# Tying GpSimd's token-number write to the place where its batch is placed, in a spectral-filter plus mixture-of-experts kernel

## The chip, the cores and the metric

The kernel runs on one core of one Trainium2 chip. The metric is the device time of one execution in microseconds (us), less is better; three runs of the kernel before stand as its measurement.

## What is computed

The input is eight batches of 2496 rows by 256 columns. Each batch is filtered in the frequency domain, and every filtered row (a token, 19968 in all) goes through one of eight experts:

```python
X = np.fft.rfft(x, axis=1)
y = np.fft.irfft(X * (filt_r + 1j * filt_i)[None], n=2496, axis=1)
t = y.reshape(19968, 256)
logits = t @ w_gate + modality_bias[modality_id]
e = argmax(logits, axis=1)                  # one expert of 8
gate = softmax(logits)[arange(N), e]
out = gate[:, None] * (relu(t @ w1[e]) @ w2[e])
```

## The kernel before

**Stages.** The transforms are matrix products on TensorE (PE): stage 1, then stage 2 (forward, filter on VectorE, inverse), then stage 3, with two DRAM tensors `b1_d` and `b2_d` between them for the later batches. Stage 3 of batch g fills a row tile `yw` (`yo0` for even g, `yo1` for odd g, in the order listings `yo_105` and `yo_106`) of 128 partitions by 20 rows. A row of it is 130 words: 128 words hold the 256 fp16 values of a token, one word its token number, and one its gate weight.

**Routing.** After stage 3 of a batch, `counting(g)` on VectorE (DVE) finds each token's expert and a running count `c`. `placing(g)` has PE sum `c` over the partitions (`psO`, lines 637 and 638), and DVE works out from it the row `pos_i` of each token in the bins (line 652). At its head GpSimd (POOL) writes the 2560 token numbers of the batch into the row tile: `tok` plus `g * S`, line 635, once for each batch. `scatter(g, t)` (line 678) then sends column t of the row tile into `bins_d` in DRAM by an indirect DMA that POOL issues; there are 20 of these for each batch, 160 in all. They are called bins-scatters below.

**Experts.** The bins are read back in blocks of 256 tokens of one expert (`xs`, issued by SyncE). `turn` transposes a block (`pT`, then DVE's copy `xT`, line 786) and copies the expert's first matrix (line 777); `up` (line 799) and `down` (line 812) are the two products, in four steps a block. At the end of a block DVE multiplies by the gate into `osb` (line 819, twice a block), and POOL issues two indirect DMAs that put the rows into the output (line 821, the out-scatters). `osb` has three buffers: DVE may write the one of block k + 3 when the out-scatters of block k have landed. `ops`, the sum in PSUM, has two.

**Order.** All engines run their instructions in the order of their queues. In the main loop (lines 1136 to 1170) each turn n does a step of stages 1 to 3 of several batches, one or two bins-scatters (`pace`) and 1.5 steps of experts. The order in each queue is made at build time by a scheduler that looks at dependences. An instruction on POOL that depends on nothing recent may be put far ahead of its place in the program. To hold DMAs back, the kernel has `paced` (line 130), which adds a dependence on the last PE matmul that was recorded so far in `marks["pe"]`:

```python
def paced(ins):
    tc.add_manual_dep(ins.ins, marks["pe"][-1].name, ..., reason="pace")
```

Weight loads (line 450), some x loads and the bins-scatters (line 686) are paced. Line 635 is not: it depends on `tok` and on the row tile alone. Its first two executions have nothing to wait for but the set-up use of these tiles. From batch 2 on it waits until the bins-scatters of batch g - 2, which read the same row tile, have landed in DRAM.

Of the kernel before, what the change touches and what calls it, by code (L numbers as in the profile page):

```python
# [16 lines left out]
ALU = mybir.AluOpType  # L17
# [12 lines left out]
def kernel(  # L30
# [12 lines left out]
    nc = tc.nc  # L43

    B, S, D = x.shape
# [31 lines left out]
    DW = D // 2  # L77
# [52 lines left out]
    def paced(ins):  # L130
        tc.add_manual_dep(ins.ins, marks["pe"][-1].name,
                          mybir.DependencyInfo(mybir.DependencyClass.Sync, mybir.DependencyReason.DATA),
                          reason="pace")
# [18 lines left out]
    op = ctx.enter_context(tc.tile_pool(name="opsum", bufs=1, space=bass.MemoryType.PSUM))  # L152
# [477 lines left out]
    def placing(g):  # L630

        yw, lg = st[g]["yw"], st[g]["lg"]
        b3 = [P, NY, E]
        mx, ohT, sc, c = st[g]["route"]
        nc.gpsimd.tensor_single_scalar(yw[:, :, DW:DW + 1], tok, g * S, op=ALU.add)
        psO = pp.tile([P, 2, E], F32, tag="ps")
        nc.tensor.matmul(psO[:, 0, :], lhsT=Lexcl, rhs=c, start=True, stop=True)
        nc.tensor.matmul(psO[:, 1, :], lhsT=ones_sq, rhs=c, start=True, stop=True)
        nc.vector.tensor_sub(lg, lg, mx[:, :, None].to_broadcast(b3))
        nc.scalar.activation(lg, lg, AF.Exp)  # L640
        off = sp.tile([P, E], F32, tag="off")
        nc.vector.tensor_add(off, cnt, ecap)
        nc.vector.tensor_add(off, off, psO[:, 0, :])
        nc.vector.tensor_add(cnt, cnt, psO[:, 1, :])
        yield
        nc.vector.tensor_add(sc, sc, off[:, :, None].to_broadcast([P, E, NY]))
        nc.vector.tensor_mul(sc, sc, ohT)
        yield
        pos = sp.tile([P, NY], F32, tag="pos")
        nc.vector.reduce_sum(pos, sc.rearrange("p e t -> p t e"), axis=AX.X)  # L650
        pos_i = sp.tile([P, NY], I32, tag="posi", bufs=2)
        nc.vector.tensor_copy(pos_i, pos)
        st[g]["pos"] = pos_i
        yield
        ssum = sp.tile([P, NY], F32, tag="ssum")
        nc.vector.reduce_sum(ssum, lg, axis=AX.X)
        nc.vector.reciprocal(yw[:, :, DW + 1].bitcast(F32), ssum)
# [10 lines left out]
    def place(g):  # L668

        run(placing(g))  # L670
# [277 lines left out]
    with tc.manual_schedule(engines={ET.PE, ET.Activation, ET.DVE}):  # L948
# [92 lines left out]
        tok = const_pool.tile([P, NY, 1], I32)  # L1041
# [36 lines left out]
        def routes(g):  # L1078

            yield from counting(g)  # L1080
            for _ in range(4):
                yield
            yield from placing(g)
            to_bins.append([g, 0])
            yield
            yield from tabling(g, KR[g], False)
# [127 lines left out]
```

## Time and profile before

| what | value |
|---|---|
| three runs, median (lowest to highest) | 594.89 us (594.38 to 596.47) |
| the profiled execution's own time | 592.98 us |
| its span, first to last instruction | 591.2 us |
| busy: PE, DVE, ACT, POOL | 512.1, 377.6, 379.9, 367.4 us |
| granted TensorE clock, mean share of full speed | 0.941 |
| bins-scatters (line 678) | 160, mean 1013 ns |
| out-scatters (line 821) | 158, mean 1014 ns |
| token-number writes (line 635) | 8, 3.1 us busy, 21.3 us idle ahead of them |

A busy time is the sum of an engine's instructions. Idle time is put down to what ended it. The clock is the share of full speed that TensorE was granted; 1.0 is 2.4 GHz and 0.5 is 1.2 GHz.

### The profile page before, as it was taken

How to read it: one execution, taken by the hardware profiler on the slowest of the kernel's cores; microseconds unless marked ns; L12 is line 12 of the kernel's file. 1: busy time of each engine (PE TensorE's matmuls, PEld its weight loads, DVE VectorE, ACT ScalarE, POOL GpSimd, SP SyncE). 2: the span in 40 equal slices, each digit the busy share in tenths (PEclk: the TensorE clock that was granted, in tenths of full speed). 3: DMA queues.
4: the chain of work that ended last, by engine and by line, in shares of the span. 5: the costliest groups of instructions: out<-in, count | busy, mean ns of one | idle time of the engine just before them, and what ended most of it. 6: DMA issues, size and time to landing. Idle time of an engine off the chain costs nothing.

```text
span 591.2 us, 16242 instructions
## 1 busy us (share of the span) xinstructions
PE 512.1 (87%) x5115; PEld 463.2 (78%) x5115; DVE 377.6 (64%) x1209; ACT 379.9 (64%) x693; POOL 367.4 (62%) x409
## 2 busy tenths in 40 slices
PE   3689986739969989999999989966999999999991
PEld 2677875628858888888888978855999999999991
DVE  8557986656766777769679777554555555555541
ACT  4578886827856877777876754433666666666660
POOL 8112336727746776774776776777777777655552
PEclk9969998969998998999998999978999999999997
DMA  8949999887697787898667463224444443333321
GB/s 152 184 68 192 197 212 208 180 204 209 160 239 208 203 198 222 231 211 241 184 176 204 139 165 112 87 86 146 137 127 123 119 125 122 118 109 110 99 73 33
DMA packets 69301, 93.29 MB, mean 158 GB/s; under 512 B 11427, under 2 KB 52841, under 8 KB 69059
## 3 DMA queue, kind: packets, MB, share of 16 engines
q0 software_dynamic: 21504, 50.75, 35.2%
q1 hardware_dynamic: 24409, 29.94, 20.1%
q10 hardware_dynamic: 23302, 11.50, 7.4%
q8 instruction: 48, 0.79, 0.6%
q14 instruction: 38, 0.31, 0.2%
HBM read 64.68 MB, written 46.35 MB: 188 GB/s over the span
## 4 chain that ended last, share of the span: by engine, by line
PE 46%; DMA 20%; issue 11%; POOL 9%; DVE 8%; ACT 3%; SPq 0%; POOLq 0%; DVEq 0%; ACTq 0%
PE hps L799 14%; PE ops L812 13%; POOL out_dram L821 5%; DMA t<-b_d 5%; DMA b_d<-t 3%; DMA bins_d<-yo,pos_i 3%; DMA b_d<-z 3%; PE ps L476 3%; DMA out_dram<-osb,meta 2%; DMA g<-g 2%; PE pz L488 2%; PE lt L584 2%; PE ps L569 2%; PE pz L489 2%; PE pT L785 2%
## 5 line engine op out<-in xcount | busy, mean ns | idle before, releaser
L804 ACT ACTIVATE hT<-hps 128x512 f16<-128x512 f32 x316 | 188.1, 597 | 120.7 <-PE hps L799 118.7
L799 PE MATMUL hps<-xT,w 128*128 128x256 f16 x1264 | 203.6, 282 | 5.7 <-DVE xT L786 5.6
L821 POOL DMA_INDIRECT out_dram<-osb,meta x158 | 160.1, 1014 | 76.4 <-DVE osb L819 36.6
L812 PE MATMUL ops<-w2sb,hT 128*128 x1264 | 198.5, 277 | 2.7 <-issue 2.5
L678 POOL DMA_INDIRECT bins_d<-yo,pos_i x160 | 162.1, 1013 | 56.6 <-issue 19.8
L799 PEld LDWEIGHTS <-w 128*128 128x128 f16 x1264 | 148.1, 146 | 11.0 <-DVE xT L786 6.0
L812 PEld LDWEIGHTS <-hT 128*128 128x128 f16 x1264 | 125.2, 99 | 18.9 <-issue 3.1
L819 DVE TENSOR_SCALAR osb<-ops,meta 128x256 f32<-128x256 f32 x158 | 69.4, 475 | 24.9 <-DMA out_dram<-osb,meta 17.3
L777 DVE COPY w<-w1sb 128x2048 f16 x79 | 56.2, 711 | 42.9 <-PE hps L799 41.1
L786 DVE COPY xT<-pT 128x512 f16<-128x512 f16 x79 | 33.4, 423 | 53.0 <-PE pT L785 52.3
L503 ACT CAST xf<-ps 104x512 f16<-104x512 f32 x96 | 56.9, 592 | 11.5 <-PE ps L476 9.5
L510 DVE TENSOR_TENSOR p<-xf,g 104x512 f16<-104x512 f16 x96 | 40.5, 421 | 36.7 <-ACT xf L503 35.8
L525 ACT CAST z<-pz 104x512 f16<-104x512 f32 x72 | 42.5, 590 | 9.7 <-PE pz L489 8.1
L476 PE MATMUL ps<-t,w2m 104*104 104x256 f16 x192 | 39.9, 292 | 8.7 <-DMA t<-b_d 7.9
L511 DVE TENSOR_TENSOR xf<-xf,g 104x512 f16<-104x512 f16 x96 | 40.5, 421 | 10.0 <-DMA g<-g 6.9
L488 PE MATMUL pz<-p,a1m 104*104 104x256 f16 x144 | 37.5, 284 | 2.7 <-DVE p L510 1.8
L218 ACT CAST t<-ps 96x512 f16<-96x512 f32 x52 | 30.1, 581 | 14.3 <-PE ps L214 12.8
L593 DVE COPY yT<-lt 128x512 f16<-128x512 f16 x80 | 33.5, 419 | 7.1 <-PE lt L589 6.3
L489 PE MATMUL pz<-xf,a2m 104*104 104x256 f16 x144 | 36.6, 280 | 0.0
L785 PE MATMUL pT<-ident,xs 128*128 128x128 f16 x316 | 32.8, 227 | 4.4 <-DMA xs<-bins_d 4.4
L144 POOL DMA_DIRECT2D xt<-in_x_dram x32 | 18.3, 573 | 28.7 <-PE fp L253 14.2
L584 PE MATMUL lt<-ident,yo 128*128 128x128 f16 x320 | 31.4, 221 | 3.7 <-ACT z L525 3.3
(206 smaller groups left out, 725.5 us busy)
## 6 DMA issues: line engine op xcount, KB each, us to landing
xs<-bins_d SPq DMA_DIRECT2D x79, 130.0 KB
xt<-in_x_dram POOLq DMA_DIRECT2D x24, 384.0 KB
t<-b_d SPq DMA_DIRECT2D x18, 384.0 KB
t<-b_d SPq DMA_DIRECT2D x15, 416.0 KB
b_d<-z ACTq DMA_DIRECT2D x30, 208.0 KB
b_d<-t ACTq DMA_DIRECT2D x24, 192.0 KB
w1sb<-in_moe_w_dram POOLq DMA_DIRECT2D x16, 256.0 KB
w2sb<-in_moe_w_dram POOLq DMA_DIRECT2D x8, 512.0 KB
```

Of the source, the lines that this page charges most:

```text
L476: mm = nc.tensor.matmul(ps[:KB, i, :], lhsT=w2m[:, s + i, :], rhs=st[g]["t2", s // SCH][:, s % SCH + i, :], start=True, stop=True)
L488: nc.tensor.matmul(pz[:KB, i, :], lhsT=a1m[:, s + i, :], rhs=p1[:, i, :], start=True, stop=False)
L489: nc.tensor.matmul(pz[:KB, i, :], lhsT=a2m[:, s + i, :], rhs=p2[:, i, :], start=False, stop=True)
L503: nc.scalar.copy(xf, ps[:KB])
L678: ins = nc.gpsimd.indirect_dma_start(out=bins_d[:, :], out_offset=IOA(ap=st[g]["pos"][:rows, t:t + 1], axis=0), in_=st[g]["yw"][:rows, t, ...
L777: cp = nc.vector.tensor_copy(b["w1"].rearrange("p a f -> p (a f)"), w1sb[:, ds(ej, 1)].rearrange("p o a f -> p (o a f)"))
L785: nc.tensor.transpose(pT[:, dc, i, :], xh[:, i, dc * P:(dc + 1) * P], ident)
L799: mm = nc.tensor.matmul(hps[:, k, :], lhsT=b["w1"][:, dc, ft:F:FT], rhs=b["xT"][:, dc].rearrange("p i t -> p (i t)"), start=(dc == 0), sto ...
L804: nc.scalar.activation(b["hT"][:, q * FQ:(q + 1) * FQ, :], hps, AF.Relu)
L812: nc.tensor.matmul(b["ops"][:, i, :], lhsT=b["hT"][:, ft, i * P:(i + 1) * P], rhs=w2sb[:, ds(b["ej"], 1), ft, :], start=(ft == 0 and i == ...
L819: nc.vector.tensor_scalar_mul(osb[:, i, :], b["ops"][:, i, :], gate[:, i, :])
L821: ins = nc.gpsimd.indirect_dma_start(out=out[:, :], out_offset=IOA(ap=b["meta"][:, i, 0:1], axis=0), in_=osb[:, i, :], in_offset=None, bou ...
```

## The change

The write of the token numbers gets the same dependence as the bins-scatters: it waits for the last PE matmul that was recorded before its batch was placed. Nothing else in the program is changed.

```diff
@@ placing(g) @@
         mx, ohT, sc, c = st[g]["route"]
-        nc.gpsimd.tensor_single_scalar(yw[:, :, DW:DW + 1], tok, g * S, op=ALU.add)
+        paced(nc.gpsimd.tensor_single_scalar(yw[:, :, DW:DW + 1], tok, g * S, op=ALU.add))
         psO = pp.tile([P, 2, E], F32, tag="ps")
```

The queues of PE, DVE, ACT and SyncE hold the same instructions in the same order as before, with waits on the same semaphores. Only POOL's queue differs. In the pieces below, rows with a minus are of the kernel before and rows with a plus of the changed one; the bracket names the semaphores that an instruction waits for (DMASW0 to DMASW7: DMAs that POOL issued; PE, DVE, Activation, Pool: these engines).

POOL's queue where the bins-scatters of batch 3 (from `yo_106`) end and those of batch 4 (from `yo_105`) begin:

```order
 L678 DMA bins_d<-yo_106,pos_i 162048x130 [waits DMASW2_49,PE_49]
-L635 TENSOR_SCALAR yo_106<-tok 128x20 [waits DMASW6_49,DMASW5_49,DMASW7_49,DMASW4_49,DMASW2_49]
 L144 DMA xt<-in_x_dram 96x512 [waits DMASW3_49,PE_49]
-L821 DMA out_dram<-osb,meta 19968x256 [waits DVE_49]
-L678 DMA bins_d<-yo_105,pos_i 162048x130 [waits DVE_49,PE_49,Pool_49]
-L678 DMA bins_d<-yo_105,pos_i 162048x130
+L635 TENSOR_SCALAR yo_105<-tok 128x20 [waits PE_49]
+L821 DMA out_dram<-osb,meta 19968x256 [waits DMASW4_49,DVE_49]
+L678 DMA bins_d<-yo_105,pos_i 162048x130 [waits DMASW5_49,DVE_49,Pool_49]
+L678 DMA bins_d<-yo_105,pos_i 162048x130 [waits DMASW6_49]
```

Before, the write that stands here is the one of batch 5, into the tile that batch 3 has just been sending out, and it waits for five DMA semaphores. In the changed queue it is the write of batch 4, into the other tile, and it waits for PE.

POOL's queue where batch 5 (`yo_106`) ends and batch 6 (`yo_105`) begins:

```order
 L678 DMA bins_d<-yo_106,pos_i 162048x130 [waits DMASW7_49]
-L635 TENSOR_SCALAR yo_106<-tok 128x20 [waits DMASW5_49,DMASW6_49,DMASW2_49,DMASW7_49,DMASW1_49,DMASW0_49]
-L821 DMA out_dram<-osb,meta 19968x256 [waits DVE_49] x2
-L678 DMA bins_d<-yo_105,pos_i 162048x130 [waits DVE_49,PE_49,Pool_49]
+L635 TENSOR_SCALAR yo_105<-tok 128x20 [waits PE_49]
+L821 DMA out_dram<-osb,meta 19968x256 [waits DMASW0_49,DVE_49]
+L821 DMA out_dram<-osb,meta 19968x256 [waits DMASW1_49,DVE_49]
+L678 DMA bins_d<-yo_105,pos_i 162048x130 [waits DMASW2_49,DVE_49,Pool_49]
```

Here the write of batch 7 gives its place to the write of batch 6. The same holds one batch earlier, where batch 4 ends and batch 5 begins.

POOL's queue where the bins-scatters of batch 6 have ended and those of batch 7 begin:

```order
 L821 DMA out_dram<-osb,meta 19968x256 [waits DMASW6_49,DVE_49]
 L821 DMA out_dram<-osb,meta 19968x256 [waits DMASW7_49,DVE_49]
-L821 DMA out_dram<-osb,meta 19968x256 [waits DMASW0_49,DVE_49]
-L821 DMA out_dram<-osb,meta 19968x256 [waits DMASW1_49,DVE_49]
-L678 DMA bins_d<-yo_106,pos_i 162048x130 [waits DVE_49,DMASW2_49,PE_49,Pool_49]
+L635 TENSOR_SCALAR yo_106<-tok 128x20 [waits PE_49]
+L821 DMA out_dram<-osb,meta 19968x256 [waits DMASW0_49,DVE_49]
+L821 DMA out_dram<-osb,meta 19968x256 [waits DMASW1_49,DVE_49]
+L678 DMA bins_d<-yo_106,pos_i 162048x130 [waits DMASW2_49,DVE_49,Pool_49]
```

Before, no write stands here any more. In the changed queue the write of batch 7 comes here, ahead of the out-scatters of one block.

## Rows read from the trace of the kernel before

**Rows 1.** The page, busy time and share of the span of each engine.

```profile
PE 512.1 (87%) x5115; PEld 463.2 (78%) x5115; DVE 377.6 (64%) x1209; ACT 379.9 (64%) x693; POOL 367.4 (62%) x409
```

**Rows 2.** Who waited for whom, POOL, 181 to 504 us: total, times, longest.

```profile
POOL yo L635 <- DMA bins_d<-yo,pos_i: 16.4, 4, 6.4
...
POOL out_dram L821 <- DVE osb L819: 7.6, 24, 0.5
```

**Rows 3.** The timeline of POOL: start, duration, instruction, idle time before and its releaser.

```profile
124.70 0.29 POOL L635 TENSOR_SCALAR yo<-tok 128x20 int32<-128x20 int32 x1 [4.74 <-DMA bins_d<-yo,pos_i]
130.12 1.05 POOL L678 DMA_INDIRECT bins_d<-yo,pos_i  x1 [5.13 <-DVE take L737]
...
276.06 0.32 POOL L635 TENSOR_SCALAR yo<-tok 128x20 int32<-128x20 int32 x1 [6.41 <-DMA bins_d<-yo,pos_i]
...
277.47 1.30 POOL L821 DMA_INDIRECT out_dram<-osb,meta  x1 [0.30 <-DVE yT L593]
...
320.25 0.28 POOL L635 TENSOR_SCALAR yo<-tok 128x20 int32<-128x20 int32 x1 [2.72 <-DMA bins_d<-yo,pos_i]
...
323.65 0.97 POOL L678 DMA_INDIRECT bins_d<-yo,pos_i  x1 [0.30 <-PE pT L785]
...
363.74 0.28 POOL L635 TENSOR_SCALAR yo<-tok 128x20 int32<-128x20 int32 x1 [2.89 <-DMA bins_d<-yo,pos_i]
...
367.13 0.98 POOL L678 DMA_INDIRECT bins_d<-yo,pos_i  x1 [0.30 <-PE lt L589]
...
394.90 1.02 POOL L821 DMA_INDIRECT out_dram<-osb,meta  x1 [0.30 <-DVE xT L786]
...
404.07 1.00 POOL L821 DMA_INDIRECT out_dram<-osb,meta  x1 [0.30 <-issue]
...
434.02 0.98 POOL L821 DMA_INDIRECT out_dram<-osb,meta  x1 [0.30 <-DVE meta L789]
```

**Rows 4.** Who waited for whom, whole span: the waits of DVE's gate product.

```profile
DVE osb L819 <- DMA out_dram<-osb,meta: 17.3, 8, 5.5
```

**Rows 5.** The timeline of DVE: gate products and the bins' positions.

```profile
271.66 0.47 DVE L819 TENSOR_SCALAR osb<-ops,meta 128x256 f32<-128x256 f32 x1
...
315.53 0.17 DVE L652 CAST pos_i<-pos 128x20 int32<-128x20 f32 x1
...
355.79 0.17 DVE L652 CAST pos_i<-pos 128x20 int32<-128x20 f32 x1
...
384.67 0.88 DVE L819 TENSOR_SCALAR osb<-ops,meta 128x256 f32<-128x256 f32 x2 [4.41 <-DMA out_dram<-osb,meta]
...
399.00 0.88 DVE L819 TENSOR_SCALAR osb<-ops,meta 128x256 f32<-128x256 f32 x2 [2.37 <-DMA out_dram<-osb,meta]
...
407.95 0.88 DVE L819 TENSOR_SCALAR osb<-ops,meta 128x256 f32<-128x256 f32 x2 [5.51 <-DMA out_dram<-osb,meta]
...
427.83 0.86 DVE L819 TENSOR_SCALAR osb<-ops,meta 128x256 f32<-128x256 f32 x2
```

**Rows 6.** The timeline of PE: placing's sums, and the first matmuls after its idle times.

```profile
311.25 0.28 PE L637 MATMUL psO<-c,Lexcl 128*128 128x8 f32 x2
...
350.83 0.39 PE L637 MATMUL psO<-c,Lexcl 128*128 128x8 f32 x2 [0.66 <-DVE c L627]
...
388.80 0.60 PE L637 MATMUL psO<-c,Lexcl 128*128 128x8 f32 x2 [5.33 <-DVE c L627]
...
401.28 0.66 PE L799 MATMUL hps<-xT,w 128*128 128x256 f16 x4 [1.18 <-DVE xT L786]
...
409.37 1.07 PE L799 MATMUL hps<-xT,w 128*128 128x256 f16 x4 [3.94 <-DVE xT L786]
```

**Rows 7.** Busy time in stretches: length, PE (matmuls), PEld, DVE, ACT, POOL, clock, DMA.

```profile
389.00:396.00 7.00, 7.00 (x42) 5.73 (x43) 3.82 (x20) 1.84 (x4) 5.39 (x6) 0.59 0.25 77
...
410.00:416.00 6.00, 6.00 (x36) 4.71 (x34) 1.71 (x6) 2.07 (x4) 4.48 (x6) 0.56 0.48 149
416.00:450.00 34.00, 34.00 (x327) 31.78 (x325) 18.71 (x48) 21.56 (x37) 26.07 (x27) 1.00 0.41 124
```

## The prediction

> **What bounds the kernel now.** I read the busy times first, then POOL's waits, then the timelines of POOL, DVE and PE side by side. By busy time PE is the engine that counts, with 87% of the span against 62% for POOL [rows 1]. That is an average over stages. Between 181 and 504 us POOL works through its queue without a pause worth the name: 24 waits for `osb` come to 7.6 us with none over 0.5 us, which is the 0.30 us step from one DMA to the next. The one exception is the token-number write, 16.4 us in four waits, each for the bins-scatters just issued to land [rows 2]. So in this stretch POOL is behind, and whatever holds it makes it later still.
>
> Who suffers? DVE writes `osb` into three buffers and waits for the out-scatter of three blocks earlier. These waits are 17.3 us in 8 times in the whole run [rows 4], and the three long ones lie at 385, 399 and 408 us, with 4.41, 2.37 and 5.51 us [rows 5]. DVE runs in order, so its stand at 385 us delays the count `c`, on which PE then stands for 5.33 us; the other two delay `xT`, on which PE stands for 1.18 and 3.94 us [rows 6]. After the first and the third the granted clock is 0.59 and 0.56 for a while, the lower level for most of it, and from 416 us on it is 1.00 with PE busy throughout [rows 7]. This is where time can be had.
>
> How late is POOL? Blocks leave DVE and POOL in the same order, so I count pairs. The `osb` of 384.67 us [rows 5] is the pair of out-scatters issued from 404.07 us [rows 3]: 19 us behind. Late in the run, where PE is never idle, the pair of 427.83 us is issued at 434.02 us, 5.3 us after its DVE instruction pair ends.
>
> **The change, part by part.** *The write itself* stays on POOL, eight times some 0.3 us [rows 3]: nothing gained or lost. *Its wait for landed scatters* goes: the write of batch g now stands at the head of batch g, and the scatters that read the same tile were those of batch g - 2, a whole batch earlier. *The added wait* is for a PE matmul recorded before the batch is placed, so it should have run before `psO`. Behind it in POOL's queue stand an x load or out-scatters, and then the bins-scatters. `psO` ran at 311.25 and 350.83 us [rows 6]; POOL came to the places at 317.5 and 360.9 us (320.25 less 2.72, 363.74 less 2.89 [rows 3]). Even if POOL comes 8 us sooner, the wait is over, so I cost it at nothing; what it costs if PE is later is the slower rival below.
>
> *What each removed wait frees on POOL.* The 4.74 us at 120 us are followed by 5.13 us for DVE's positions [rows 3]; that is late next, so zero. The fourth wait of rows 2 is 16.4 less 6.41, 2.72 and 2.89, so 4.4 us; it is over before any `osb` wait, since the first of the three long ones is at 380 us: zero. The three others add up, each up to what is late next:
> - At batch 4 the pair of 277.47 us cannot go before its `osb`, 271.66 plus 0.47 us [rows 5], plus 0.3: 272.4 us. POOL gains 5.1 us of the 6.4.
> - At batch 5 the gain would be 5.1 + 2.72 + 0.3, but the first bins-scatter (323.65 us) needs `pos_i`, ready at 315.70 us. With 0.3 it goes at 316.0 us: the gain is 7.7 us.
> - At batch 6 another 2.89 + 0.3 us give 10.9; the first scatter (367.13 us) needs `pos_i` of 355.96 us, so at best 356.3 us: 10.8 us.
>
> From there POOL's row of DMAs is the same as before, 10.8 us earlier.
>
> *What DVE and PE get from it.* The first stand (4.41 us) needs only 4.4 of the 10.8 us and vanishes. PE's 5.33 us shrink to 0.9, a gap about as long as the 0.66 and 1.18 us ones. The slow clock goes with it: 42 matmuls took 7.00 us where the later stretch needs 34.00 / 327 = 0.104 us each, so 4.4; that gives 2.6 us [rows 7]. Together 7.0. The second stand then comes at 399.00 - 2.37 - 7.0 = 389.6 us, and its buffer is free at 399.00 - 10.8 = 388.2: it vanishes, and PE's 1.18 us too. The third comes at 407.95 - 5.51 - 7.0 - 1.2 = 394.2, but its buffer is free only at 407.95 - 10.8 = 397.1 us: 2.9 of the 5.51 us stay. DVE waits have cost PE some 1.2 to 1.6 us less than their length (2.37 to 1.18, 5.51 to 3.94), so PE stands some 1.3 us, 2.6 less, without the slow stretch of 36 matmuls in 6.00 us, another 2.3. PE is ahead by 7.0 + 1.2 + 2.6 + 2.3 = 13.1 us at 416 us.
>
> But POOL is ahead by only 10.8, so its lag of 5.3 us would become 7.6. How much can three buffers bear? A buffer is free some 4 us after its pair is issued (394.90 to 399.00, 404.07 to 407.95 [rows 3, 5]). At 36 matmuls a block a block takes 3.74 us (0.104 x 36), three take 11.2, less 0.9 for the product itself and 4.0: an estimate of 6.3 us. So about 1.0 to 1.5 us of the 13.1 are given back in small `osb` waits: 10.8 + 6.3 - 5.3 = 11.8 is the ceiling. I take **11.5 us**. From there on PE is the bound in both kernels, and the gain stands to the end.
>
> *Both ends.* What no row shows is how POOL behaves when it is no longer behind: it may then wait for the PE marks of the bins-scatters. The low end is the first stand alone, 7.0 us. The high end is every PE row named, 4.4 + 2.6 + 1.2 + 3.9 + 2.3 = 14.4 us. I sit nearer the ceiling since by these sums POOL still lags by 3 us and more from 360 us on.
>
> **The numbers.** The profiled execution took 592.98 us, 1.8 around its span of 591.2. Less 11.5 that is 581.5. It lies 1.9 us under the median of the three runs, 594.89, so for the median I say **583.4 us**.
>
> **The rivals.**
> - *Everything goes* (chance 0.15): the buffers bear more than 6.3 us, or small `osb` waits stay off PE. In the stretch from 416 to 450 us PE did not stand at all, which speaks for it. 14.4 us less: 580.5.
> - *Half* (0.17): once POOL catches up, around 316 and 356 us, it waits for PE marks, and its lead at 385 us is some 6 us. The first stand goes, the rest only moves: 7 us less, 587.9. For it speaks that both `pos_i` limits bind to within 0.5 us; against it that scatters and out-scatters of a turn become ready together.
> - *No change* (0.05): PE is the bound and POOL's idle time costs nothing. For it speaks rows 1; against it that PE stood three times on DVE, behind buffers that POOL frees [rows 4 to 6]. It gives 594.9. The Trainium skill, page "Perfetto Trace Analysis", section "Identifying the Most-Contended Engine", says to take the engine of highest occupancy for the bottleneck and to work on it first. By that rule a change on POOL alone is worth nothing and the sum would be 0 instead of 11.5; the same page grants, under "Optimization Strategy", that a kernel can have several regimes, and the trace of 365 to 416 us is such a one.
> - *Slower* (0.05): the PE mark that the write now waits for passes late, because its matmul stands in PE's queue behind `psO` and more. Then POOL's whole queue stands at the write. It decides from the old landing times on: 276.06, 320.25 and 363.74 us. For every us past each, all that follows is later, and DVE's waits grow by that. Two us late at batches 5 and 6 would give 4 us more, 598.9. Against it: `psO` ran 9.0 and 12.9 us before the last two of these times [rows 3, 6].
>
> That the change does not do what it says is ruled out by the queues: at the head of batches 4 to 7 the write waits for PE alone.
>
> **How the numbers follow.** My forecast has 0.58, so faster has 0.58 + 0.15 + 0.17 = 0.90, no change 0.05 and slower 0.05. No change means within 0.3%, 1.8 us, about what a measurement of this kernel can tell. The range reaches from the first rival, with 1.5 us for the runs' scatter, to the second with 2 us: 579.0 to 590.0 us.
>
> **What would show it.** POOL's waits of line 635 for `bins_d` are gone, and the first bins-scatters of batches 5 and 6 start near 316 and 356 us, right after `pos_i`. DVE's waits of line 819 for the output fall from 17.3 us to some 3 to 6. `psO` of batch 7 stands under 1.5 us, and the clock from 383 to 416 us is near 1.00. It is wrong if line 635 waits for PE by more than 2 us where POOL lags, if PE still stands over 3 us between 380 and 416 us, or if a gap as long turns up on `t<-b_d` instead.

## The result, and the profile after

| | kernel before | changed kernel |
|---|---|---|
| median (lowest to highest), 4 runs each | 595.47 us (594.38 to 596.47) | 586.09 us (584.66 to 588.49) |
| ratio, 95% interval | 1 | 0.9847 (0.9808 to 0.9886) |
| the profiled execution's own time, span, clock | 592.98, 591.2 us, 0.941 | 588.49, 586.6 us, 0.940 |

The changed kernel is 9.4 us faster, between 6.8 and 11.4 by the interval. Its profiled execution is the longest of its four runs, 2.4 us above their median, and that of the kernel before (592.98 us) is shorter than all four of its runs, so the two profiles differ by only 4.5 us. Some executions are slower as a whole; the ratios, here and below, leave them out, so a ratio can differ from the quotient of the medians beside it (most in `e5_osb4`: 0.9846, where the medians give 0.9937).

**POOL.** The page's first part, busy time and share of the span of each engine, answers to [rows 1].

```profile
PE 508.7 (87%) x5115; PEld 460.9 (79%) x5115; DVE 375.6 (64%) x1209; ACT 379.5 (65%) x693; POOL 369.0 (63%) x409
```

PE's share reads 87% as before. POOL's waits between 181 and 504 us (waiting instruction, releaser: total, times, longest) answer to [rows 2].

```profile
POOL out_dram L821 <- DVE osb L819: 6.9, 23, 0.3
```

Line 635 has no row any more in this stretch: the 16.4 us in four waits are gone, and no wait of that line took their place there.

POOL's timeline (start, duration, instruction, idle time before and its releaser), at the places of [rows 3]:

```profile
272.54 0.29 POOL L635 TENSOR_SCALAR yo<-tok 128x20 int32<-128x20 int32 x1
274.94 1.06 POOL L821 DMA_INDIRECT out_dram<-osb,meta  x1 [2.11 <-DVE ni L705]
...
315.24 0.28 POOL L635 TENSOR_SCALAR yo<-tok 128x20 int32<-128x20 int32 x1
...
319.24 0.97 POOL L678 DMA_INDIRECT bins_d<-yo,pos_i  x1 [1.10 <-issue]
...
357.24 0.28 POOL L635 TENSOR_SCALAR yo<-tok 128x20 int32<-128x20 int32 x1
...
360.32 1.02 POOL L678 DMA_INDIRECT bins_d<-yo,pos_i  x1 [0.30 <-issue]
...
397.05 1.00 POOL L821 DMA_INDIRECT out_dram<-osb,meta  x1 [0.30 <-issue]
...
427.80 0.98 POOL L821 DMA_INDIRECT out_dram<-osb,meta  x1 [0.30 <-DVE meta L789]
```

The writes wait for nothing here. The pair of out-scatters that was issued from 404.07 us goes from 397.05 us, 7.0 us earlier; that of 434.02 us goes at 427.80 us, 6.2 earlier.

**DVE and PE.** DVE's timeline, positions and gate products, answers to [rows 5]:

```profile
318.29 0.17 DVE L652 CAST pos_i<-pos 128x20 int32<-128x20 f32 x1
...
356.94 0.21 DVE L652 CAST pos_i<-pos 128x20 int32<-128x20 f32 x1
...
381.51 0.87 DVE L819 TENSOR_SCALAR osb<-ops,meta 128x256 f32<-128x256 f32 x2
...
392.63 0.87 DVE L819 TENSOR_SCALAR osb<-ops,meta 128x256 f32<-128x256 f32 x2 [1.80 <-DMA out_dram<-osb,meta]
401.81 0.88 DVE L819 TENSOR_SCALAR osb<-ops,meta 128x256 f32<-128x256 f32 x2 [5.85 <-DMA out_dram<-osb,meta]
...
421.16 0.86 DVE L819 TENSOR_SCALAR osb<-ops,meta 128x256 f32<-128x256 f32 x2
```

PE's timeline, the first matmuls after its idle times, answers to [rows 6]:

```profile
231.57 0.28 PE L569 MATMUL ps<-t,wbm 96*128 96x256 f16 x1 [2.92 <-DMA t<-b_d]
...
352.73 0.39 PE L637 MATMUL psO<-c,Lexcl 128*128 128x8 f32 x2 [0.82 <-DVE c L627]
...
385.71 0.39 PE L637 MATMUL psO<-c,Lexcl 128*128 128x8 f32 x2 [0.83 <-DVE c L627]
...
394.86 0.66 PE L799 MATMUL hps<-xT,w 128*128 128x256 f16 x4 [0.67 <-DVE xT L786]
...
403.07 0.66 PE L799 MATMUL hps<-xT,w 128*128 128x256 f16 x4 [4.09 <-DVE xT L786]
```

The stand of 4.41 us at 384.67 us is gone (the product runs at 381.51 us without one), and PE's 5.33 us for `c` are 0.83. The second (2.37, PE 1.18) is 1.80 (PE 0.67). The third has stayed: 5.85 us where it was 5.51, PE 4.09 where it was 3.94. In the whole span DVE's waits for the output fell from 17.3 us [rows 4] only to 13.2:

```profile
DVE osb L819 <- DMA out_dram<-osb,meta: 13.2, 6, 5.8
```

The windows (length, PE, PEld, DVE, ACT, POOL busy with counts, clock, DMA share, GB/s) answer to [rows 7]:

```profile
389.00:396.00 7.00, 6.33 (x59) 5.66 (x58) 4.69 (x17) 3.97 (x7) 5.17 (x7) 1.00 0.33 105
400.00:406.00 6.00, 2.93 (x17) 2.30 (x18) 2.75 (x7) 1.20 (x2) 4.78 (x5) 0.81 0.49 154
405.00:411.00 6.00, 6.00 (x51) 5.34 (x50) 1.38 (x4) 2.99 (x5) 4.48 (x6) 0.82 0.53 165
416.00:450.00 34.00, 34.00 (x328) 31.98 (x327) 18.75 (x48) 21.66 (x37) 26.37 (x26) 1.00 0.40 124
```

After the first place the granted clock is now 1.00, where it was 0.59; after PE's stand of 4.09 us it still falls, to 0.81.

**One loss lies ahead of all this.** The first row of PE's fence is a stand of 2.92 us at 228.65 us, for a load of `t`, where the kernel before had none. PE runs `psO` of batch 4 at 271.77 us, 2.5 us later than before (269.24), and `pos_i` of batch 5 is ready 2.8 us later.

**The stretch by itself.** What lies ahead moves from profile to profile, so the stretch is best measured between two of its own marks: from `psO` of batch 6 (350.83 us before [rows 6], 352.73 now) to the gate product of the block behind the stands (427.83 us before [rows 5], 421.16 now). It took 77.0 us and takes 68.4, which is 8.6 us less. The changed kernel comes to its start 1.9 us late, so 6.7 us are left at its end.

Nine of the twelve runs below were made on chips where every kernel, the one before too, had a median of 714 to 734 us; they are compared only with the kernel before on the same chip.

### The profile page after: what moved, and what is told of

The parts are those of the page before. It is cut to its first block, busy times and chain, and to the rows that moved or that the text cites. A ratio compares the mean times of both kernels' runs of the same rounds, so it can differ in the third digit from the quotient of the medians.

```text
span 586.6 us, 16249 instructions
## 1 busy us (share of the span) xinstructions
PE 508.7 (87%) x5115; PEld 460.9 (79%) x5115; DVE 375.6 (64%) x1209; ACT 379.5 (65%) x693; POOL 369.0 (63%) x409
## 4 chain that ended last, share of the span: by engine, by line
PE 52%; DMA 17%; issue 10%; POOL 8%; DVE 6%; ACT 3%; SPq 1%; POOLq 0%; DVEq 0%; ACTq 0%
PE hps L799 15%; PE ops L812 15%; POOL out_dram L821 5%; DMA t<-b_d 4%; DMA b_d<-t 4%; PE ps L569 3%; PE ps L476 3%; PE lt L584 3%; DMA bins_d<-yo,pos_i 2%; PE pz L488 2%; PE ps L572 2%; DMA g<-g 2%; PE pz L489 2%; PE pT L785 2%; DMA b_d<-z 2%
## 5 line engine op out<-in xcount | busy, mean ns | idle before, releaser
L678 POOL DMA_INDIRECT bins_d<-yo,pos_i x160 | 163.9, 1024 | 66.8 <-issue 21.7
L819 DVE TENSOR_SCALAR osb<-ops,meta 128x256 f32<-128x256 f32 x158 | 69.3, 474 | 20.2 <-DMA out_dram<-osb,meta 13.2
L569 PE MATMUL ps<-t,wbm 96*128 96x256 f16 x120 | 30.4, 283 | 4.9 <-DMA t<-b_d 4.8
```

The source lines that it names most:

```text
L569: mm = nc.tensor.matmul(ps[:, i, :], lhsT=wbm[:, 0, :], rhs=t4[:, t - t0, :], start=True, stop=u0 >= NYF)
L678: ins = nc.gpsimd.indirect_dma_start(out=bins_d[:, :], out_offset=IOA(ap=st[g]["pos"][:rows, t:t + 1], axis=0), in_=st[g]["yw"][:rows, t, ...
L819: nc.vector.tensor_scalar_mul(osb[:, i, :], b["ops"][:, i, :], gate[:, i, :])
```

## The experiments

The theory: before the change POOL was late from batch 4 on, its lateness reached DVE through the three `osb` buffers, and PE stood on DVE at three places; so only the writes that waited after 270 us (those of batches 5, 6 and 7) count. Rivals: any wait removed from POOL counts; the gain comes by another way than `osb`; the write itself, or its being moved, matters.

### Only the late writes tied, or only the early ones

`e6_late`:

```diff
-        paced(nc.gpsimd.tensor_single_scalar(yw[:, :, DW:DW + 1], tok, g * S, op=ALU.add))
+        (paced if g >= 5 else id)(nc.gpsimd.tensor_single_scalar(yw[:, :, DW:DW + 1], tok, g * S, op=ALU.add))
```

> The late writes alone once more (batches 5, 6 and 7 tied, 0 to 4 early), since the first run of it was made where every kernel took some 23% longer and DVE did not wait for osb at all. Theory, where the kernel before takes some 595 us: the whole gain, 585 to 588 us, within 1.5 us of the changed kernel, because only the landing waits near 276, 320 and 364 us reach DVE. Rival (the gain comes from the early stretch): 593 to 596 us. Where the kernel before takes some 730 us again, POOL is not late and neither theory says more than 0 to 5 us.

`e12_early` is the same line with `g < 5`:

> Only the writes of batches 0 to 4 are tied; those of batches 5, 6 and 7 stay where they stood in the kernel before, at the end of batches 3, 4 and 5, and wait there for landed scatters. My theory says that a wait on POOL counts only where POOL's lateness reaches the osb buffers: the waits that this takes away (4.74 us at 120 us and 4.4 us near 224 us in the profile of before, 9.1 us together) lie too early and are worth nothing, while the three that stay (12 us together) keep the stands at 385 to 408 us. So DVE's waits for the output stay at 14 to 18 us, PE still stands 4 us and more near 385 us, and the ratio to the kernel before is 0.997 to 1.003. The rival, that every removed wait on POOL counts about alike, gives 9.1 of 21 us of removed waits, so some 4 us, a ratio of 0.991 to 0.995.

| | median, runs | before, same chip | ratio, 95% interval |
|---|---|---|---|
| late writes | 587.60 us, 9 | 593.85 us | 0.9889 (0.9851 to 0.9926) |
| early writes | 592.16 us, 12 | 593.96 us | 0.9984 (0.9944 to 1.0023) |

The late writes alone bring 6.3 us; the early ones nothing that can be told from no change. Both take waits away: in the profile of `e12_early` two waits for landed scatters are gone and three stay, 11.2 us. POOL's waits of line 635 for the bins, 181 to 504 us, in `e12_early`:

```profile
POOL yo L635 <- DMA bins_d<-yo,pos_i: 11.2, 3, 6.3
```

The same row in `e6_late`, where one early wait of the stretch stays:

```profile
POOL yo L635 <- DMA bins_d<-yo,pos_i: 4.1, 1, 4.1
```

PE's timeline of `e12_early` (`psO` of batch 6 first) keeps all three stands:

```profile
347.58 0.39 PE L637 MATMUL psO<-c,Lexcl 128*128 128x8 f32 x2 [0.58 <-DVE c L627]
...
384.74 0.59 PE L637 MATMUL psO<-c,Lexcl 128*128 128x8 f32 x2 [4.77 <-DVE c L627]
...
397.66 0.66 PE L799 MATMUL hps<-xT,w 128*128 128x256 f16 x4 [1.28 <-DVE xT L786]
...
405.93 1.07 PE L799 MATMUL hps<-xT,w 128*128 128x256 f16 x4 [4.15 <-DVE xT L786]
```

In that of `e6_late` the first has shrunk, as in the changed kernel, and the third has stayed:

```profile
349.36 0.39 PE L637 MATMUL psO<-c,Lexcl 128*128 128x8 f32 x2 [0.70 <-DVE c L627]
...
381.56 0.39 PE L637 MATMUL psO<-c,Lexcl 128*128 128x8 f32 x2 [0.98 <-DVE c L627]
...
391.24 0.66 PE L799 MATMUL hps<-xT,w 128*128 128x256 f16 x4 [1.27 <-DVE xT L786]
...
399.06 1.07 PE L799 MATMUL hps<-xT,w 128*128 128x256 f16 x4 [3.71 <-DVE xT L786]
```

The gate product of the block behind the stands, in DVE's timeline of `e12_early`:

```profile
424.15 0.87 DVE L819 TENSOR_SCALAR osb<-ops,meta 128x256 f32<-128x256 f32 x2
```

The same product in `e6_late`:

```profile
417.69 0.87 DVE L819 TENSOR_SCALAR osb<-ops,meta 128x256 f32<-128x256 f32 x2
```

So the stretch from `psO` of batch 6 to this product takes 76.6 us in `e12_early` and 68.3 in `e6_late`, where the kernel before takes 77.0 and the changed one 68.4. With the late writes alone the stretch gains all that it gains with the whole change, with the early ones next to nothing.

So a wait removed from POOL counts by where it lies, not by its length. The rival that all count alike put the early writes at some 4 us, a ratio of 0.991 to 0.995; the interval begins at 0.9944, so the medians alone put it all but out. The stretch and the three stands that stay are the stronger evidence against it. By the ratios the late writes are worth 1.1%, the early ones 0.2% and the whole change 1.5%, so the parts add up within their intervals. The late ones were expected to bring the whole gain; their 6.3 us, on another chip, are two thirds of it, and the intervals of the two ratios overlap.

The profiled execution of `e6_late`, one of its shortest with 584.69 us, is one in which PE was not late at 270 us (`psO` of batch 4 at 269.08). Its POOL timeline tests the prediction's times one by one:

```profile
272.24 1.07 POOL L821 DMA_INDIRECT out_dram<-osb,meta  x1 [2.18 <-DVE ni L705]
...
316.01 0.97 POOL L678 DMA_INDIRECT bins_d<-yo,pos_i  x1 [0.85 <-issue]
...
393.47 1.00 POOL L821 DMA_INDIRECT out_dram<-osb,meta  x1 [0.30 <-issue]
...
423.93 0.99 POOL L821 DMA_INDIRECT out_dram<-osb,meta  x1 [0.31 <-DVE meta L789]
```

### A fourth osb buffer on top of the change

`e11_osb4`:

```diff
-        sc = sp.tile([P, E, NY], F32, tag="sc")
+        sc = sp.tile([P, E, NY], F32, tag="oh")
...
-            osb = ep.tile([P, NI, D], F32, tag="osb", bufs=3)
+            osb = ep.tile([P, NI, D], F32, tag="osb", bufs=4)
```

> The changed kernel with a fourth osb buffer, so that DVE may write the osb of block k + 4 when the out-scatters of block k have landed (to make room, sc takes turns with another tile, which may cost waits on DVE). My theory says that after the change POOL is still 13 to 15 us late near 385 us, that DVE therefore still stands some 13 us for osb and PE once for 4 us near 400 us, and that three buffers are what passes POOL's lateness on. A fourth one lets POOL be one more block (some 4 us) late: DVE's waits for the output fall from 13 us to under 6, PE's stand of 4.1 us near 400 us falls under 1.5 us, and the time is 2 to 5 us less than the changed kernel's, a ratio to the kernel before of 0.977 to 0.983. First rival, that the change gained by something else than osb: DVE's waits change little and the ratio stays at 0.985 or is higher. Second rival, that POOL itself is the bound in this stretch: DVE's waits for osb go, but as many us of waits on the last blocks turn up later between 416 and 450 us, ratio 0.985. If the whole kernel runs about a fifth slower on PE than in the profile of before, POOL is not late at all, and the ratio is 0.995 to 1.0.

Measured: 582.25 us (574.03 to 585.10, 6 runs) against 593.22, ratio 0.9777 (0.9687 to 0.9867). That is faster than the kernel before, and inside the range that was expected. Against the changed kernel's 0.9847 the intervals overlap, so by the medians it is likely and not shown that it beats it. Its profile has a span of 580.1 us. DVE's waits for the output in the whole span:

```profile
DVE osb L819 <- DMA out_dram<-osb,meta: 11.3, 7, 4.5
```

DVE's timeline, gate products from 391 us on:

```profile
391.02 0.86 DVE L819 TENSOR_SCALAR osb<-ops,meta 128x256 f32<-128x256 f32 x2
...
399.39 0.88 DVE L819 TENSOR_SCALAR osb<-ops,meta 128x256 f32<-128x256 f32 x2 [4.53 <-DMA out_dram<-osb,meta]
...
408.35 0.88 DVE L819 TENSOR_SCALAR osb<-ops,meta 128x256 f32<-128x256 f32 x2 [1.68 <-DMA out_dram<-osb,meta]
...
412.47 0.88 DVE L819 TENSOR_SCALAR osb<-ops,meta 128x256 f32<-128x256 f32 x2 [2.02 <-DMA out_dram<-osb,meta]
...
414.76 0.88 DVE L819 TENSOR_SCALAR osb<-ops,meta 128x256 f32<-128x256 f32 x2 [0.35 <-DMA out_dram<-osb,meta]
```

PE's timeline, `psO` of batch 6 and the one stand of over 1 us between 380 and 416 us:

```profile
351.54 0.39 PE L637 MATMUL psO<-c,Lexcl 128*128 128x8 f32 x2 [0.77 <-DVE c L627]
...
400.77 0.66 PE L799 MATMUL hps<-xT,w 128*128 128x256 f16 x4 [2.44 <-DVE xT L786]
```

The marks were too bold: DVE's waits fell by 1.9 us, not by 7, and PE's stand from 4.09 to 2.44 us, not under 1.5. The fourth buffer moves the long wait one block on, from the block of 401.81 us in the changed kernel to that of 399.39 us here, and lets POOL be later: the block whose product starts at 414.76 us is issued at 425.06 us, 10.3 us after; in the changed kernel the same block starts at 421.16 us and is issued at 427.80, 6.6 after. Small waits follow to 434 us. But they don't take the lead back, as the second rival had it: at the product of 414.76 us this kernel is 13.1 us ahead of the kernel before, at its last product 13.0 (565.95 and 578.92 us). The stretch from `psO` of batch 6 takes 63.2 us, 5.2 less than in the changed kernel, in this one profile. So the buffers pass POOL's lateness on. What is late is POOL itself, which issues one DMA every 1.3 us (1.0 us busy and the 0.30 us step) without a pause here.

### The runs on the chips with medians of 714 to 734 us

`e1_again` and `e7_again` are the changed kernel. `e2_late` is `e6_late`; `e3_early` and `e8_early` are `e12_early`; `e5_osb4` and `e9_osb4` are `e11_osb4`. The two others:

```diff
-        paced(nc.gpsimd.tensor_single_scalar(yw[:, :, DW:DW + 1], tok, g * S, op=ALU.add))
+        g < 2 and nc.gpsimd.tensor_single_scalar(yw[:, :, DW:DW + 1], tok, g * S, op=ALU.add)
```

(`e4_no_write`, which leaves the token numbers of batches 2 to 7 unwritten), and, with every write of batches 5 and 6 done twelve times (`e10_dose`):

```diff
-        paced(nc.gpsimd.tensor_single_scalar(yw[:, :, DW:DW + 1], tok, g * S, op=ALU.add))
+        [paced(nc.gpsimd.tensor_single_scalar(yw[:, :, DW:DW + 1], tok, g * S, op=ALU.add)) for _ in range(12 if g in (5, 6) else 1)]
```

> The changed kernel once more, for a second profile and a closer ratio. Theory (POOL's lag reaches DVE through the three osb buffers): 9 to 11 us under the kernel before, line 635 waits under 3 us in the stretch from 165 to 504 us, psO of batch 7 makes PE stand under 1.5 us, and one stand of 3 to 4.5 us on xT stays near 400 us. Open: PE's stand of 2.9 us on t<-b_d near 229 us in the first profile of the changed kernel, which the kernel before does not have. If the change brings it, it is here again with over 2 us; if it is chance, it is under 1 us.

> Only the writes of batches 5, 6 and 7 are tied to their place; those of 0 to 4 stand early as before, so the landing waits near 124 and 224 us stay and those near 276, 320 and 364 us go. Theory: the whole gain, 585 to 588 us, within 1.5 us of the changed kernel. Rival (the gain comes from the early stretch, from the waits near 124 and 224 us or from DMAs that moved there): 593 to 596 us.

> The counterpart: only the writes of batches 0 to 4 are tied; those of 5, 6 and 7 stand early, so the three late landing waits stay. Theory: no gain, 593.5 to 597 us, with osb waits of 15 us or more on DVE. Rival (gain from the early stretch): 585 to 588 us.

> Leaves out the write of the token numbers from batch 2 on (the rows then go to the rows of earlier batches); neither the landing wait nor the new wait for PE is there, and every DMA is issued as before. Theory (the new wait costs nothing that matters): within 1.5 us of the changed kernel, 584.5 to 587.5 us. Rival (the new wait at the head of POOL's queue eats part of the gain): 582 to 584 us.

> The changed kernel with four osb buffers in place of three (room for it by letting the running count sc use the buffer of oh, which is dead by then; the order of all queues stays). Theory (what is left of POOL's lag still reaches DVE through three buffers, 13.2 us of waits, and makes PE stand for 4.1 us near 399 us with a slow clock behind it): the osb waits for landed out-scatters fall under 4 us and the kernel gains another 3 to 7 us, to a ratio of 0.973 to 0.980 to the kernel before. Rival (the waits of osb don't matter, the gain came another way): within 1 us of the changed kernel, a ratio near 0.985.

> The changed kernel again, beside the next three on one chip. Theory: 8 to 11 us under the kernel before, where that takes some 595 us; psO of batch 7 makes PE stand under 1.5 us; one stand on xT near 400 us stays. PE's stand on t<-b_d near 229 us: over 2 us again if the change brings it, under 1 us if the first profile had it by chance.

> The early writes alone: batches 0 to 4 tied, 5 to 7 early, so that the landing waits near 276, 320 and 364 us stay. Theory: at most 2 us of gain, 592 to 596 us where the kernel before takes 594, with osb waits of 14 us or more on DVE. Rival (a good part of the gain comes from the early stretch): 3 us or more of gain, 586 to 591 us.

> The changed kernel with four osb buffers (sc shares the buffer of oh). Theory (what is left of POOL's lag still reaches DVE through three buffers): the waits of osb for landed out-scatters fall from 13 us to under 5, PE's stand near 399 us and the slow clock behind it go, and the kernel gains another 3 to 7 us: 578 to 583 us, a ratio of 0.973 to 0.981. Rival (osb waits don't matter): within 1.5 us of the changed kernel.

> The changed kernel in which the writes of batches 5 and 6 are done twelve times over, which keeps POOL busy some 3.5 us more at each of the two places and adds no wait for a landing. Theory (POOL's lateness as such is what counts): 4 to 7 us of the gain are given back, 590 to 593 us, with osb waits of 14 us or more. Rival (what counted was the wait for landed bins-scatters, or where DMAs fall): 585 to 588 us, as the changed kernel.

| run | median us | before | ratio, 95% interval |
|---|---|---|---|
| e1_again | 724.15 | 732.85 | 0.9881 (0.9831 to 0.9931) |
| e2_late | 728.36 | 732.85 | 0.9962 (0.9922 to 1.0003) |
| e3_early | 730.81 | 732.85 | 0.9961 (0.9923 to 0.9999) |
| e4_no_write | 725.11 | 732.85 | 0.9891 (0.9848 to 0.9934) |
| e5_osb4 | 728.85 | 733.45 | 0.9846 (0.9793 to 0.9899) |
| e7_again | 715.72 | 716.80 | 0.9978 (0.9943 to 1.0012) |
| e8_early | 719.26 | 716.80 | 0.9961 (0.9916 to 1.0006) |
| e9_osb4 | 714.68 | 716.80 | 1.0007 (0.9970 to 1.0044) |
| e10_dose | 718.58 | 716.80 | 1.0009 (0.9971 to 1.0046) |

Their profiles say why they settle little. The page of `e7_again` (span 706.9 us), busy times:

```profile
PE 555.4 (79%) x5115; PEld 481.4 (68%) x5115; DVE 377.4 (53%) x1209; ACT 377.3 (53%) x693; POOL 362.7 (51%) x409
```

PE takes 46.7 us longer for the same 5115 matmuls and is idle for 151.5 us, where the changed kernel's profile above has 77.9; what slows it on these chips is open. POOL's waits, 181 to 504 us:

```profile
POOL out_dram L821 <- DVE osb L819: 23.6, 12, 4.8
```

And DVE's waits of line 819 that end on a DMA, in the same stretch:

```profile
DVE osb L819 <- DMA xt<-in_x_dram: 0.2, 1, 0.2
DVE osb L819 <- DMA bins_d<-yo,pos_i: 0.2, 1, 0.2
```

So POOL is not late there: POOL waits for `osb`, up to 4.8 us at a time, and DVE for no out-scatter; none of the nine profiles has a wait of line 819 for one. Then the theory gives nothing to gain, and on the chip of the last four runs nothing was gained (0.9978), nor lost by 22 writes more (1.0009). On that of the first four the changed kernel still gained 1.2% (0.9881), and leaving the later writes out gave as much (0.9891). That agrees with the write itself costing nothing, but by what way the 1.2% came there is open. The two halves of the change gave 0.4% each (0.9962 and 0.9961), which together lie within its interval. The same edit gave 0.9846 and 1.0007 with four buffers on two chips; these nine runs are not used for a size. The two tests of POOL's lateness by dose and of the write itself (`e10_dose`, `e4_no_write`) were made there alone, so what they would give where POOL is late is not shown. That the write costs nothing there rests on the changed kernel's trace, in which it waits for nothing from 181 to 504 us.

## Why the prediction was right, and which terms were off

The sign and the cause were right. The size was 9.4 us where 11.5 were forecast; 586.09 us lies between the forecast's 583.4 and the rival "half" (587.9), and nearer to the rival. What PE did is also what that rival says: the first stand goes, and the third only comes earlier. Its reason is not seen, since no write waited for a PE mark there; POOL waited for `osb` and `pos_i`. That the time lies in the range owes something to the room that the rivals gave it.

- **The write and its added wait cost nothing**: right. Its only waits for PE in the whole span are 3.0 and 1.5 us, both ahead of 168 us, where POOL is not late.
- **The waits at 120 and 224 us are worth nothing**: right, as far as `e12_early` can tell (0.9984, 0.9944 to 1.0023).
- **What POOL gains at batches 4, 5 and 6**: `osb` at batch 4 and `pos_i` at batch 5 were limits as named. In `e6_late` the three times came out at 272.24, 316.01 and 393.47 us; predicted were 272.4, 316.0 and 404.07 - 10.8 = 393.3. In the changed kernel's profile they are 274.94, 319.24 and 397.05, since PE, and with it `osb` and `pos_i`, were 2.5 to 2.8 us late there after the stand at 228.65 us. At batch 6 `pos_i` was no limit: the first bins-scatter came 3.2 us after it in both profiles (353.80 to 356.97 us in `e6_late`, 357.15 to 360.32 in the changed kernel). At batch 5 it came 0.78 us after `pos_i` in both, where 0.3 was put, so that 316.01 us met the forecast is luck in part: `pos_i` was 0.5 us earlier in `e6_late`. That POOL's lead hangs on how early PE makes `pos_i` of batch 5 is the prediction's own reasoning; that PE's place at 270 us can move by itself was not in it.
- **The first stand vanishes, 5.33 to 0.9, and the slow clock after it**: right, 0.83 us and 1.00. **The second** is 0.67 instead of nothing (1.27 in `e6_late`).
- **The third keeps 2.9 of 5.51 us, PE some 1.3**: wrong. It kept 5.85 and 4.09 us, and the 2.3 us for the clock after it came only in part (0.82 where it was 0.56). This is the step that failed. DVE arrived for this buffer at 401.81 - 5.85 = 395.96 us, and the buffer came free when POOL's pair of 397.05 us had landed, 4.8 us after its start (3.9 before). The forecast had DVE here at 394.2 us and the buffer free at 397.1. The buffer came 4.7 us later than that, and 3.8 of it is POOL's lead, 7.0 us and not 10.8. In `e6_late` POOL is 10.6 us ahead, but DVE is also further ahead (392.39 us), and the wait is 5.41 us. In both profiles what PE gained beyond POOL's lead was stood out here. Put with PE's rows the sum reads 4.5 (5.33 to 0.83) + 2.6 + 0.5 (1.18 to 0.67) - 0.2 (3.94 to 4.09) and a part of 2.3, so 7.4 to 9.7 us, and the stretch gained 8.6.
- **The buffers bear 1 us more than POOL's lead (11.8 is the ceiling)**: a little too high. By the product of 421.16 us (427.83 before) DVE leads by 6.7 us and POOL's pair by 6.2; in `e6_late` both lead by 10.1. The lead after the stands is POOL's lead, with half a us on top at most.
- **From there PE is the bound, and the gain stands to the end**: right for PE, which stands nowhere after 416 us by over 0.6 us. But the profiles' spans differ by less than their last products: the changed kernel's is 6.6 us earlier, its span 4.6 us shorter. The end has a length of its own, below.
- **The marks of failure**: the text named "PE still stands over 3 us between 380 and 416 us", and it did. It failed as a mark, since a stand shows only that DVE is ahead of POOL there, not that nothing was gained. The gap "as long" on `t<-b_d` also came in part (2.92 us). Of the marks of success, DVE's waits did not fall to some 3 to 6 us but to 13.2, and the clock was not near 1.00 to 416 us (0.81 and 0.82 from 400 to 411 us).
- **The rule of occupancy** (the Trainium skill, page "Perfetto Trace Analysis", section "Identifying the Most-Contended Engine") points to PE, and it is PE's stands that shrank. Read as the rival reads it, that a change on POOL alone is worth nothing, it fails here: POOL has 63% of the span, PE 87% and its weight loads 79%, and 9.4 us came from a change in POOL's queue alone.

## What to carry to other kernels

An engine that is busy 62% of the span can be behind in one stage; look there for a queue without pauses, count how far it runs behind its partner, and see which buffers pass that on. A wait removed from such a queue is worth what is left of it when it reaches the buffers: here waits of 9 us ahead of the stage gave nothing that could be told from no change, and those of 12 us inside it some 6 us. The gain is capped by what the late queue needs next (here `pos_i` of batch 5) and by its own pace. A stand further on that hangs on the same queue need not shrink: here PE's third one only came 6.3 us earlier.

## What the runs showed of the hardware that was not expected

- **A stand that comes and goes.** PE's wait for `t` near 228 us was 0 in the profiles of before and of `e12_early`, and 1.63, 1.76 and 2.92 us in `e6_late`, `e11_osb4` and the changed kernel. None of the nine profiles on the other chips has it at this line. Its cause is open. The moved writes don't make it, since up to there `e6_late` has POOL's queue in the order of the kernel before. The change leaves SyncE's queue as it was: in the changed kernel an `xs` load, which needs the last bins-scatter of batch 2, is issued at 224.25 us and the first load of `t` behind it at 225.49; the kernel before has them at 224.40 and 225.64 us, and no stand.
- **An end of two lengths.** From the start of the last out-scatter to the end of the span it took 9.4 us before (581.77 to 591.2) and 11.5 after (575.13 to 586.6). In the profiles of the twelve runs it is 9.4 us three times (`e2_late`, `e9_osb4`, `e10_dose`) and 10.7 to 11.6 us nine times, which follows no edit.
- **Runs scatter by 8 to 10 us** on one chip (583.85 to 591.47 for `e6_late`, 588.11 to 597.89 for `e12_early`), more than the early writes could be worth; single profiles show where time goes, medians how much.
